# Adaptive-norm attention and spatial-shift MLP on one core: TensorE's order chosen by the state of banks and engines

## The chip, the cores and the metric

One Trainium2 chip, one of its cores. The metric is the device time of one execution in microseconds. The engines are named as the profile names them: PE (TensorE, matrix products), DVE (VectorE), ACT (ScalarE), POOL (GpSimd) and SP (SyncE, which issues the DMAs here). PE writes its results into PSUM banks, from which DVE and ACT read.

## The reference

The input x has 2048 rows of 512. A row of modulation vectors is made from c; then come an attention block with 32 heads of 16, and a mixer with a shift along the sequence, followed by an MLP of width 1792. Between them stand layer norms.

```python
mod = (silu(c) @ w_mod).reshape(1, 6, 1, -1)          # sa, ca, ga, sb, cb, gb
h = layernorm(x) * (1 + ca) + sa
q, k, v = split(h @ wqkv)                             # 32 heads of 16
x = x + ga * (softmax(q @ k.T * 16 ** -0.5) @ v) @ wo
h = layernorm(x) * (1 + cb) + sb
g = gelu(layernorm(h) @ w1)                           # tanh form
x1 = h + concat(shift(g, 1), shift(g, -1), shift(g, 2), shift(g, -2)) @ w2
x = x + gb * (x1 + gelu(layernorm(x1) @ w3) @ w4)
```

Weights are scaled up (by 8 in the attention, by 64 in the mixer), so that products are made of high and low parts: three matmuls (lines 339, 341 and 343, the helper mm3) for one exact product.

## The kernel before

All instructions are recorded in an order that a planner (class Sched) works out while the kernel is built. It keeps one modelled clock per engine (T["P"] for PE, "A" for ACT, "D" for DVE, "G" for POOL, "S" for the DMA queue), chains of dependent operations that wait for those clocks, and generators that yield PE work. On the chip each engine then takes its instructions strictly in the recorded order.

The program has three stages. First layer norm and the first keys and queries. Then a long stage in which attention runs and all other products (the rest of q, k, v; wo, w1, w2, w3, w4 for the four chunks of 512 rows) are placed between its parts. At the end what is left of the last chunk.

Attention runs over 64 units (four chunks of 512 queries by 16 pairs of heads) with 16 steps each, 1024 steps in all. Step s has two row pairs (row_pair). A row pair is two matmuls that run together on the two halves of PE's rows: sc (line 1021) for the scores of step s, and mb (line 1005), the same scores turned round, 24 steps ahead (LEAD), of which DVE takes the maximum (line 1001, mx<-mb) so that a unit's shift is known before its scores come. ACT then takes exp of sc (line 1017, pt<-sc). p_low halves the upper parts of pt, on POOL (line 1072) or, when POOL is late by the plan, in two halves on ACT (line 127). The columns (pv_part) are four matmuls at a time: with the high parts (line 1098, one for each step) and with the low parts (line 1095, one for two steps), so three parts for two steps.

sc and mb share seven PSUM banks (NSM) with the other products. A row pair takes two banks; they come free when DVE has its maximum and ACT its exp.

What sets PE's order around the change is a fixed pattern. The main loop walks over blocks of three row pairs (GRP). Each block is recorded whole: it waits until the plan has banks for all its pairs (sch.gap fills that wait with other products), then come three pairs, then, in every second block (CPER), all column parts that are two blocks back (LAG), and in the other blocks sch.fill places other products up to a budget of nanoseconds for each step (SC0, TAILB). At some steps drain forces the generators on until a key is done.

```python
    blocks = [range(32 * u + i, min(32 * u + i + GRP, 32 * u + 32)) for u in range(-2, NU) for i in range(0, 32, GRP)]
        if k >= LAG and (k % CPER == 0 or not blk):
        if k % CPER == CPER - 1 or s0 < 0:
            sch.fill(due)
```

The elementwise work of the other products also runs through the planner: a gelu is Square on ACT, cube on DVE, Tanh on ACT, prod on DVE, then a copy and a difference for the two parts on ACT and POOL; x1_add, xb_add and z_add (lines 1372, 1482, 1535) add a finished product on DVE. The factor 0.5 of gelu is put into w2 and w4 by an extra ACT copy of each of their 18 half pieces (line 899).

## Time and profile before

| what | value |
|---|---|
| median of 3 runs | 2002.66 us (2001.76 to 2005.11) |
| the profiled execution, from its first to its last instruction | 2000.7 us, mean granted clock 0.986 |
| PE busy | 1920.9 us (96%) |
| DVE busy | 1652.2 us (83%) |
| ACT busy | 1473.6 us (74%) |
| POOL busy | 1676.1 us (84%) |
| stage with rows and columns | 61.5 to 1845.6 us |

Busy time of an engine is the time in which at least one of its instructions runs. Matmuls are pipelined, and one that waits inside the pipeline counts as busy; what PE really needs is better read from the distance between the starts of its matmuls. The line number in a row leads to the code; names on both sides of the arrow are what an instruction writes and reads. A row "A <- B" of the waits says that A stood idle until B was done.

### The profile page before, as it was taken

The page shows a single profiled execution, that of the slowest core. Times are in us where ns is not written, and L with a number is a line of the kernel's source. Part 1 is how long each engine was busy: PE and PEld are TensorE (multiplying, and loading weights), DVE is VectorE, ACT ScalarE, POOL GpSimd, SP SyncE. Part 2 cuts the span into 40 slices and gives each one's busy share as a digit, 9 for nine tenths or more (in the row PEclk, how much of TensorE's full clock was granted, in tenths as well). Part 3 has the DMA queues.
Part 4 walks back from the last instruction along what each step waited for, and adds up shares of the span by engine and source line. Part 5 has one row for each costly group of instructions (what it writes and reads, how often), then busy time and mean ns, then how long its engine had stood idle before and what let it go on. Part 6 is the DMA issues. An engine that isn't in the chain of part 4 may idle for free.

```text
span 2000.7 us, 42354 instructions
## 1 busy us (share of the span) xinstructions
PE 1920.9 (96%) x14480; PEld 1146.7 (57%) x14480; DVE 1652.2 (83%) x3010; ACT 1473.6 (74%) x3083; POOL 1676.1 (84%) x1609
## 2 busy tenths in 40 slices
PE   7999999999999999999999999999999999999899
PEld 4655555555455555555455555555555555555798
DVE  7887988888899888888989898898898889883643
ACT  5376888777878777777878787786787878777443
POOL 6287999889999998888999998898899989888532
PEclk8999999999999999999999999999999999999999
DMA  5767677766643334345433333334433343334432
GB/s 184 205 201 228 182 231 218 244 225 192 198 157 111 115 103 143 109 136 162 126 111 92 109 111 114 115 119 148 157 98 100 115 151 107 121 95 147 149 146 90
DMA packets 232352, 293.24 MB, mean 147 GB/s; under 512 B 125876, under 2 KB 177076, under 8 KB 215848
## 3 DMA queue, kind: packets, MB, share of 16 engines
q1 hardware_dynamic: 232136, 290.53, 46.4%
q8 instruction: 115, 1.88, 0.4%
q14 instruction: 101, 0.83, 0.1%
HBM read 225.81 MB, written 62.91 MB: 144 GB/s over the span
## 4 chain that ended last, share of the span: by engine, by line
PE 67%; DVE 16%; ACT 8%; issue 3%; POOL 2%; DMA 2%; SPq 1%; POOLq 0%; ACTq 0%; DVEq 0%
PE mb L1005 14%; PE sc L1021 10%; PE pv L1098 10%; DVE mx L1001 9%; PE w L339 7%; PE w L343 6%; PE w L341 6%; PE pv L1095 4%; ACT pt L1017 4%; POOL pt L1072 2%; DVE xs L1421 1%; DVE sq L1418 1%; DMA vst<-Vs 1%; PE mr L644 1%; PE ot L1127 1%
## 5 line engine op out<-in xcount | busy, mean ns | idle before, releaser
L1072 POOL TENSOR_SCALAR pt<-pt 128x1024 f16<-128x1024 uint16 x988 | 1312.5, 1365 | 132.6 <-ACT pt L1017 125.4
L1001 DVE TENSOR_REDUCE mx<-mb 128x1 f32<-128x512 f32 x2048 | 1281.0, 683 | 76.0 <-PE mb L1005 54.5
L1017 ACT ACTIVATE pt<-sc 128x512 int32<-128x512 f32 x2048 | 1090.8, 606 | 272.3 <-PE mb L1005 164.9
L1005 PE MATMUL mb<-kst,qtl 64*128 64x512 f32 x2048 | 752.1, 454 | 49.0 <-ACT pt L1017 16.1
L1021 PE MATMUL sc<-qtl,kst 64*128 64x512 f32 x2048 | 716.4, 444 | 2.6 <-DVE A L329 0.6
L1005 PEld LDWEIGHTS mb<-kst,qtl 64*128 64x128 f32 x2048 | 348.7, 193 | 254.5 <-DVE mx L1001 91.4
L1021 PEld LDWEIGHTS sc<-qtl,kst 64*128 64x128 f32 x2048 | 335.6, 186 | 153.5 <-DVE mx L1001 47.1
L1098 PE MATMUL pv<-pt,vst 128*32 128x512 f16 x4096 | 358.2, 397 | 0.1
L1095 PE MATMUL pv<-pt,vst 128*17 128x512 f16 (+1 forms) x2048 | 213.7, 394 | 2.2 <-POOL pt L1072 1.7
L1098 PEld LDWEIGHTS <-vst 128*32 128x32 bf16 x4096 | 90.9, 95 | 167.6 <-issue 108.8
L339 PE MATMUL w<-A,wr 128*128 128x256 f32 (+2 forms) x576 | 175.3, 304 | 0.3 <-ACT A L333 0.3
L1428 POOL TENSOR_TENSOR g<-xs,g 128x256 fp32r<-128x256 f32 (+2 forms) x144 | 103.2, 718 | 83.4 <-ACT g L1427 81.3
L341 PE MATMUL w<-A,wr 128*128 128x256 f32 (+2 forms) x576 | 169.8, 295 | 0.5 <-DVE A L329 0.3
L343 PE MATMUL w<-A,wr 128*128 128x256 f32 (+2 forms) x576 | 167.7, 291 | 0.0
L339 PEld LDWEIGHTS w<-A,wr 128*128 128x128 f32 x576 | 109.6, 190 | 35.4 <-DVE mx L1001 10.3
L339 PE MATMUL w<-wr,g 128*128 128x512 f32 x288 | 119.2, 414 | 0.6 <-ACT g L1427 0.6
L341 PEld LDWEIGHTS w<-A,wr 128*128 128x128 f32 x576 | 109.9, 191 | 12.4 <-issue 11.3
L343 PE MATMUL w<-wr,g 128*128 128x512 f32 x288 | 114.7, 398 | 0.2 <-POOL g L1428 0.2
L341 PE MATMUL w<-wr,g 128*128 128x512 f32 x288 | 113.6, 394 | 0.0
L343 PEld LDWEIGHTS w<-A,wr 128*128 128x128 f32 x576 | 109.8, 191 | 6.7 <-issue 6.7
L1535 DVE TENSOR_TENSOR x<-x,w 128x512 f32<-128x512 f32 x64 | 43.9, 687 | 82.0 <-PE w L343 82.0
L1424 ACT ACTIVATE sq<-w 128x256 f32<-128x256 f32 (+2 forms) x144 | 55.7, 387 | 68.8 <-PE w L343 66.0
(151 smaller groups left out, 2103.8 us busy)
## 6 DMA issues: line engine op xcount, KB each, us to landing
wr<-Ws SPq DMA_DIRECT2D x80, 1024.0 KB
kst<-Ks SPq DMA_DIRECT2D x189, 256.0 KB
vst<-Vs SPq DMA_DIRECT2D x252, 192.0 KB
qtl<-Qs SPq DMA_DIRECT2D x192, 64.0 KB
Vs<-vt SPq DMA_DIRECT2D x32, 384.0 KB
Ws<-wq SPq DMA_DIRECT2D x40, 256.0 KB
Ws<-wst SPq DMA_DIRECT2D x40, 256.0 KB
wst<-in_B_w_dram SPq DMA_DIRECT2D x36, 256.0 KB
```

What stands on the lines that cost most here:

```text
L339: te.matmul(o, lh, rh, start=first, stop=False)
L341: te.matmul(o, lh, rl, start=False, stop=False)
L343: te.matmul(o, ll, rh, start=False, stop=last)
L1001: end = sch.crit("D", 605, e + PX, lambda: dve.reduce_max(mxs[u][:, j, g, c:c + 1], b, axis=AX.X))
L1005: return ready, lambda: te.matmul(b, lhs, kst[u % 3][r, c * CH:(c + 1) * CH], start=True, stop=True), after
L1017: ea = sch.crit("A", 480, e + PX, lambda: act.activation(pt[s][:, j], b, AF.Exp))
L1021: return ready, lambda: te.matmul(b, kst[u % 3][r, kt * P:(kt + 1) * P], qst[u][r], start=True, stop=True), after
L1072: e_low[s] = XP["G"] + sch.crit("G", 1345, ready, lambda: pool.tensor_scalar(o, i, 0.5, 1.0, op0=OP.mult, op1=OP.mult))
L1095: te.matmul(acc[r:r + n, :], v[:, (kt + i) % 4, c - n:c].bitcast(F16), pt[s + i].bitcast(F16)[:, j, 0::2], start=False, stop=kt == NKT - 2 ...
L1098: te.matmul(acc[r:r + 32, :], v[:, kt % 4, r:r + 32], pt[s].bitcast(F16)[:, j, 1::2], start=kt == 0, stop=False, skip_group_check=True)
L1424: sch.chain(("A", cA(n), lambda: act.activation(sq, b, AF.Square)), ("D", cD(n), cube), ("A", cA(n), lambda: act.activation(sq, sq, AF.Tan ...
L1428: ("G", cG(n), lambda: pool.tensor_tensor(lo, xs, hi, op=OP.subtract)), (None, 0, end), bank=b)
```

## The change

- The main loop has no blocks. It holds three modes for PE (r rows, c columns, o other products), and Sched.to books 95 ns for each change and 107 more for an entry into rows. At each turn it looks at the modelled banks and clocks. Inside a burst of rows (up to GRP pairs) it goes on while the next pair's banks come free within STAY (300 ns). Otherwise it reckons when banks for a whole burst are free (st) and when the engine that drains them runs dry (dry); rows start if that is not more than BACK (150 ns) away, and not while many column parts are ready or much credit for other products is left. Until then it places columns, if at least CMIN (4) parts are ready or if they fit into the time left, or else other products, while there is credit.
- Credit for other products follows DUES: pairs of a step and of the microseconds that are to be spent on them by then, 67.7 by step 20 up to 527.8 by step 1012. SC0 and TAILB go.
- p_low is recorded one pair of steps later (PLAG) and one row at a time; the second half on ACT follows after the next row.
- A unit's loads (load_unit) may come up to UWAIT (4) steps later, where the products that they read are not stored yet; before, drain forced them at once. The drain for oT at the start of a chunk becomes a wait inside o_fin, and o_fin's tiles sm and rc have one buffer more each.
- The factor 0.5 of gelu moves into the normalization ahead of w1 and w3: the variance is multiplied by 4 in an instruction that stands there already, Square and Tanh get scales of 2, and the 18 ACT copies go.
- The zero rows of qtl are copied from a tile of 4 by 128 that is read four times, where it was 4 by 512.

```diff
-SC0 = (32, 900.0, 700.0)
-TAILB = (0.0, 500.0, 560.0, 590.0)
+DUES = ((20, 67.7), (60, 87.3), (85, 95.9), (122, 115.8), (150, 130.7), (205, 149.7), (245, 167.7),
+        (505, 270.0), (765, 395.7), (1012, 527.8))
+BTOP, BLOW = 1200.0, 300.0
...
+SWITCH, ENTER = 95.0, 107.0
+EARLY, STAY, BACK, GRACE = 300.0, 300.0, 150.0, 0.0
+OWE, CTOP = 500.0, 5000.0
+CHIGH, CMIN, CMOST, PTLOW, PLAG = 2500.0, 4, 6, 2, 1
...
+    def to(self, mode):
+        if self.mode != mode:
+            self.T["P"] += SWITCH + (mode == "r") * ENTER
+            self.mode = mode
...
-            if nm in ("w2", "w4"):
-                ops.append(("A", cA(), lambda f=f: act.activation(f, f, AF.Copy, scale=0.5)))
...
+            yield lambda: not ci or ("oT", ci - 1) in done
...
-        sm = at.tile([P, 8, DH + 1], F32, name="sm", tag="sm", bufs=1)
-        rc = at.tile([P, 8, 1], F32, name="rc", tag="rc", bufs=2)
+        sm = at.tile([P, 8, DH + 1], F32, name="sm", tag="sm", bufs=2)
+        rc = at.tile([P, 8, 1], F32, name="rc", tag="rc", bufs=3)
...
-                dve.tensor_scalar(mv[:, 1:2], mv[:, 1:2], EPS, None, op0=OP.add)
+                dve.tensor_scalar(mv[:, 1:2], mv[:, 1:2], EPS, 4.0 if half else 1.0, op0=OP.add, op1=OP.mult)
...
-            sch.chain(("A", cA(n), lambda: act.activation(sq, b, AF.Square)), ("D", cD(n), cube),
-                      ("A", cA(n), lambda: act.activation(sq, sq, AF.Tanh, scale=GELU_A * GELU_C)),
+            sch.chain(("A", cA(n), lambda: act.activation(sq, b, AF.Square, scale=2.0)), ("D", cD(n), cube),
+                      ("A", cA(n), lambda: act.activation(sq, sq, AF.Tanh, scale=2.0 * GELU_A * GELU_C)),
...
+        return min(BTOP, max([BLOW] + [(1000.0 * w - sch.spent) / (d - s) for d, w in DUES if d > s]))
...
+        if asked:
+            ci, pr = units[asked[0]]
+            keys = [("kq", pr // 4)] + [("q", pr // 8)] * (ci > 0)
+            if r >= UWAIT:
+                for key in keys:
+                    drain(key)
+            if all(key in done for key in keys):
+                load_unit(asked.pop())
...
+        nc_ = cols()
+        if can:
+            if sch.mode == "r" and burst < GRP:
+                slack = one - now
+                row = slack <= STAY
+            else:
+                st = one
+                for k in range(2, GRP + 1):
+                    if need * k <= len(free) and free[need * k - 1] < LATE:
+                        st = max(st, free[need * k - 1] - (k - 1) * CROW)
+                dry = sch.T["D"] if s + LEAD < NS else sch.T["A"]
+                slack = max(st, dry - CROW - PX - EARLY) - enter - now
+                row = slack <= BACK and (sch.mode == "r" or sch.credit < CHIGH and not (nc_ >= CMIN and len(pts) <= PTLOW))
+        if not row:
+            n = 0
+            if nc_ >= CMIN or nc_ and slack >= nc_ * CCOL + (sch.mode != "c") * SWITCH:
+                do_cols(nc_)
+                n = nc_
+            else:
+                stop = now + max(slack, 0.0) + GRACE
+                while (sch.T["P"] < stop or sch.credit > CHIGH) and sch.credit > (-OVER if sch.open else 0.0) and sch.one():
+                    n += 1
...
+        if row:
+            do_row(x, max(now, one - enter))
+            burst = 1 if enter else burst + 1
+            x += 1
+            sch.credit = max(min(sch.credit + budget(s) / 2, CTOP), -OWE)
```

The numbers of instructions on PE, DVE and SP stay. In the order of the instructions the change shows at many places; three are given here. The first is PE near the end of the attention stage, before the change: from an other product (w) through two bursts of row pairs (mb and sc), with a visit to the columns (pv, each with its weights' load, of which the middle is left out) between them, to the next other product.

```order
L343 MATMUL w_27333<-wr,g_26256 128x512
L1005 MATMUL mb<-kst_153,qtl_151 128x512
L1021 MATMUL sc<-qtl_605,kst_607 128x512 x2
L1005 MATMUL mb<-kst_153,qtl_151 128x512 x2
L1021 MATMUL sc<-qtl_605,kst_607 128x512
L1098 LDWEIGHTS vst_611
L1098 MATMUL pv<-pt_614,vst_611 32x512
...
L1095 MATMUL pv<-pt_616,vst_611 25x512
L1021 MATMUL sc<-qtl_605,kst_607 128x512
L1005 MATMUL mb<-kst_153,qtl_151 128x512 x2
L1021 MATMUL sc<-qtl_605,kst_607 128x512
L339 MATMUL w_27401<-wr,g_26653 128x512
```

Five column parts stand between the first two bursts, and twelve matmuls of one other product follow the second. At the same row pairs after the change:

```order
L1036 MATMUL sc<-qtl_605,kst_607 128x512
L1110 LDWEIGHTS vst_611
...
L1113 MATMUL pv<-pt_618,vst_612 32x512
L355 MATMUL w_27526<-wr,g_27111 128x512
L357 MATMUL w_27526<-wr,g_27111 128x512
L359 MATMUL w_27526<-wr,g_27111 128x512
L355 MATMUL w_27526<-wr,g_27111 128x512
L1036 MATMUL sc<-qtl_605,kst_607 128x512
L1020 MATMUL mb<-kst_153,qtl_151 128x512 x2
L1036 MATMUL sc<-qtl_605,kst_607 128x512
```

Now a few column parts and a few matmuls of an other product stand together between two bursts, and a product is cut over several such visits.

The second place is DVE at the same time before: the maxima (mx), and the adds of the other products (x).

```order
L1535 TENSOR_TENSOR x_14268<-x_14268,w_27255 128x512
L1001 TENSOR_REDUCE mx<-mb 128x1 x6
L1535 TENSOR_TENSOR x_21727<-x_21727,w_27333 128x512
L1001 TENSOR_REDUCE mx<-mb 128x1 x5
L1535 TENSOR_TENSOR x_21729<-x_21729,w_27401 128x512
L1001 TENSOR_REDUCE mx<-mb 128x1 x6
```

And after, at the adds of the products that the PE rows above show:

```order
L1016 TENSOR_REDUCE mx<-mb 128x1 x5
L1554 TENSOR_TENSOR x_13684<-x_13684,w_27486 128x512
L1016 TENSOR_REDUCE mx<-mb 128x1 x3
L1554 TENSOR_TENSOR x_21194<-x_21194,w_27526 128x512
L1016 TENSOR_REDUCE mx<-mb 128x1 x6
L1153 TENSOR_REDUCE sm<-ot 128x136
L1554 TENSOR_TENSOR x_21196<-x_21196,w_27562 128x512
```

An add stood after every fifth or sixth maximum; the distances are now less regular.

The third place is ACT in the first quarter, at the exps (pt<-sc) of about the same steps, before:

```order
L1017 ACTIVATE pt_620<-sc 128x512
L127 ACTIVATE pt_618<-pt_618 128x512
L900 ACTIVATE wq_120<-wst_116 128x512
L1017 ACTIVATE pt_620<-sc 128x512
L127 ACTIVATE pt_618<-pt_618 128x512
L1017 ACTIVATE pt_613<-sc 128x512 x2
```

And after:

```order
L1032 ACTIVATE pt_617<-sc 128x512 x2
L140 ACTIVATE pt_616<-pt_616 128x512
L914 ACTIVATE wq_120<-wst_117 128x512
L1032 ACTIVATE pt_618<-sc 128x512
L140 ACTIVATE pt_616<-pt_616 128x512
L349 ACTIVATE qk_165<-k 128x512
```

A halving on ACT comes two steps after its exp in both, in two halves with other work between them; over the program there are 120 such halves where there were 72, and POOL has 964 halvings where it had 988.

More of the change, by code (lines that the diff above doesn't have):

```diff
@@ new lines, in fillers, with do_cols, do_row @@
+    def fillers():
+        for e in "ADG":
+            sch.misc(e, max(sch.T["P"], sch.T[e]) + TOLE[e])
+    def do_cols(n):
+        sch.to("c")
+        for y in pvs[:n]:
+            if not y[1]:
+                e_hi.pop(y[0])
+            pv_part(*y)
+        del pvs[:n]
+    def do_row(x, t):
+        sch.T["P"] = t
+        sch.to("r")
+        late = sorted(e_exp)
+        one_row(x)
+        for q in late:
+            if 2 * q < x - 2 * PLAG:
+                p_low(q)
+    x, end, seen, burst = -2 * LEAD, 2 * NS, -99, 0
@@ L1632 @@
-        sch.gap(start)
-        sch.flush(need)
-        sch.T["P"] = max(sch.T["P"], start) + CIN
-        low = sorted(e_exp)
-        for s, i in row:
-            for fn in row_pair(s, i):
-                fn()
+        can = x < end
+        if can:
+            s, i = divmod(x, 2)
+            if x == LENDS:
+                sch.most = MOST
+            if i == 0 and seen != s:
+                seen = s
+                before(s)
+                if s >= 0 and s % 16 == 0:
+                    drain(("shift", s // 16))
+            can = i or s < 0 or bool(pts)
@@ L1639 @@
+        now, row, slack = sch.T["P"], False, LATE
+        if can:
+            need = (s >= 0) + (s + LEAD < NS)
+            sch.flush(need)
+            free = sorted(sm.t)
+            one = free[need - 1 + 2 * (s < 0)]
+            if one >= LATE:
+                one = free[need - 1]
+            enter = (sch.mode != "r") * (SWITCH + ENTER)
+        else:
+            for q in sorted(e_exp):
+                p_low(q)
             while second:
                 second.pop(0)()
-        while second:
-            second.pop(0)()
```

117 lines of the change are left out of this document (51 added, 66 removed).

## The prediction

> **What bounds the kernel now.** I began with the page's busy shares and its chain, to see whether one engine sets the end.
>
> ```profile
> span 2000.7 us, 42354 instructions
> PE 1920.9 (96%) x14480; PEld 1146.7 (57%) x14480; DVE 1652.2 (83%) x3010; ACT 1473.6 (74%) x3083; POOL 1676.1 (84%) x1609
> PE 67%; DVE 16%; ACT 8%; issue 3%; POOL 2%; DMA 2%; SPq 1%; POOLq 0%; ACTq 0%; DVEq 0%
> ```
>
> PE looks full at 96%, yet the chain is PE's for only 67%: a matmul counts as busy while it waits in the pipeline. So the second view is PE's timeline in a clean place, read from start to start.
>
> ```profile
> start us, us, engine line op out<-in xcount [idle before <-releaser]
> 704.83 0.66 PE L1127 MATMUL ot<-ident,ac 128*128 128x128 f32 x4
> 705.24 0.50 PE L339 MATMUL w<-wr,g 128*128 128x512 f32 x1
> ...
> 1752.21 0.28 PE L339 MATMUL w<-A,wr 128*128 128x256 f32 x1
> 1752.33 0.28 PE L341 MATMUL w<-A,wr 128*128 128x256 f32 x1
> ...
> 1790.35 0.39 PE L341 MATMUL w<-wr,g 128*128 128x512 f32 x1
> 1790.58 0.39 PE L343 MATMUL w<-wr,g 128*128 128x512 f32 x1
> 1790.89 0.50 PE L1005 MATMUL mb<-kst,qtl 64*128 64x512 f32 x1
> 1790.90 0.72 PE L1021 MATMUL sc<-qtl,kst 64*128 64x512 f32 x2
> 1791.24 0.61 PE L1005 MATMUL mb<-kst,qtl 64*128 64x512 f32 x2
> 1791.47 0.39 PE L1021 MATMUL sc<-qtl,kst 64*128 64x512 f32 x1
> 1791.80 0.41 PE L1098 MATMUL pv<-pt,vst 128*32 128x512 f16 x4
> 1792.03 0.41 PE L1095 MATMUL pv<-pt,vst 128*17 128x512 f16 x4
> 1792.26 0.64 PE L1098 MATMUL pv<-pt,vst 128*32 128x512 f16 x8
> 1792.72 0.42 PE L1095 MATMUL pv<-pt,vst 128*17 128x512 f16 x4
> 1793.07 0.50 PE L1021 MATMUL sc<-qtl,kst 64*128 64x512 f32 x1
> ```
>
> Here are PE's real prices. A row pair (mb and sc, which run together) takes 0.23 us (1791.24 to 1791.47), a column part (four pv) 0.23, another product 0.23 with 512 columns, 0.12 with 256, 0.10 with 128. A change between the three kinds costs more: other to rows 0.31 (1790.58 to 1790.89), rows to columns 0.33, columns to rows 0.35, so about 0.10 beyond the work. And after each entry into rows the second pair comes 0.35 after the first, another 0.11.
>
> Third, the stage and pieces of it. All row and column work lies between 61.5 and 1845.6 us.
>
> ```profile
> core 0: us, PE busy (x) PEld busy (x) DVE busy (x) ACT busy (x) POOL busy (x), PEclk, DMA share, GB/s
> 61.50:1845.60 1784.10, 1730.71 (x13482) 988.78 (x13484) 1531.93 (x2769) 1382.19 (x2899) 1579.23 (x1472) 0.99 0.48 146
> 112.00:1809.50 1697.50, 1646.73 (x12920) 936.37 (x12918) 1476.90 (x2669) 1327.89 (x2777) 1524.52 (x1418) 0.99 0.47 145
> 334.70:401.20 66.50, 61.86 (x432) 34.86 (x431) 54.81 (x83) 49.79 (x100) 55.12 (x47) 0.95 0.72 229
> 520.20:564.00 43.80, 40.72 (x330) 18.89 (x328) 40.92 (x71) 38.50 (x78) 40.96 (x36) 1.00 0.47 147
> 1651.20:1700.20 49.00, 48.40 (x414) 28.06 (x412) 45.14 (x85) 41.54 (x92) 47.56 (x44) 1.00 0.36 104
> 1700.20:1755.40 55.20, 54.82 (x439) 32.71 (x437) 46.78 (x85) 40.13 (x86) 46.44 (x42) 1.00 0.37 116
> 1809.50:1845.60 36.10, 35.22 (x294) 19.15 (x292) 9.77 (x21) 32.38 (x70) 35.33 (x35) 1.00 0.32 105
> ```
>
> By the order PE holds in that stage 2096 row slots (478 us at those prices), 1536 column parts (347), 3178 other matmuls (1062, 1480 and 636 with 512, 256 and 128 columns, 487), and 1361 changes of kind with 631 second pairs after an entry (207). That is 1519 of 1784.1 us, so PE stands still for about 265. DVE (1532) and POOL (1579) are as loaded as PE. The four rows of single pieces each hold 64 row pairs, and there are 31 such pieces from 112 to 1809.5. In 520.2 to 564.0 hardly any other product is left to place: PE needs 30, POOL (41.0) and DVE (40.9) fill the 43.8. In 1651.2 to 1700.2 POOL bounds (47.56 of 49.0), 1.4 are lost. In 1700.2 to 1755.4 PE bounds: 14.6 rows, 10.8 columns, 18.9 others, 7.2 changes, together 51.5 of 55.2, 3.7 lost. In 334.7 to 401.2 it needs 52.7 of 66.5. If I take for each piece the largest need of the four engines (counts of the order by row durations, scaled so that the whole gives the row 112 to 1809.5), the 31 pieces sum to 1566. The other 131 us are lost inside pieces, to bad timing.
>
> Fourth, who waits for PE on DVE, between 112 and 1810:
>
> ```profile
> DVE mx L1001 <- PE mb L1005: 50.9, 101, 2.0
> DVE x L1535 <- PE w L343: 47.4, 36, 1.9
> DVE mx L1001 <- PE sc L1021: 15.4, 32, 1.6
> DVE xb L1482 <- PE w L343: 10.5, 11, 1.5
> DVE x L1372 <- PE wo L343: 8.9, 12, 1.5
> 1791.00 0.69 DVE L1535 TENSOR_TENSOR x<-x,w 128x512 f32<-128x512 f32 x1 [1.50 <-PE w L343]
> ```
>
> Sum 133 us: for 66 DVE has no new bank of maxima, for 67 it stands before an add whose product PE has not finished. The last line is the pattern in small: during PE's twelve products before 1790.89 DVE is idle for 1.50 us.
>
> **The change, part by part.**
>
> Changes of kind. The new order has 1928 in place of 1361: 722 visits to rows (634), 635 to columns (352), 572 to other products (376). 567 times 0.10 is 57, and 709 second pairs in place of 631 give 78 times 0.11, or 9: **+66 us of PE time**. How much reaches the end depends on the piece. The Trainium skill, page "TensorEngine Tiling (Array Packing)", Key Properties, says that changing the tiling mode drains TensorE, and speaks so against this change; the trace agrees (64-row, 32-column and whole-array matmuls meet at those 0.10 us). The page "TensorE: Matmul & The Clock Gate", Single matmul latency, gives a lone matmul a fixed part of about 166 ns; at that price the 567 changes would be, as an estimate from that page, 94 us in place of 57.
>
> The bound of the pieces. The other products are spread more evenly: 14 to 21 us in most pieces, where before they ran from 9 to 21; the ends of chunks stay poor (four pieces with 1 to 7 us now, two with 1 and 5 before). PE's need over the 31 pieces rises from 1435 to 1511 (66 for changes, the rest other products moved forward out of the last stretch), DVE's from 1477 to 1483; POOL's falls from 1525 to 1499. The largest needs then sum to 1573 where they were 1566: **+7 us**, not 66, since in 21 of the 31 pieces PE was not the bound. It is in 15 now.
>
> The halving of pt (p_low) is part of this:
>
> ```profile
> L1072 POOL TENSOR_SCALAR pt<-pt 128x1024 f16<-128x1024 uint16 x988 | 1312.5, 1365 | 132.6 <-ACT pt L1017 125.4 <-ACT mf L1052 1.7 <-POOL pt L1072 1.1
> L127 ACT ACTIVATE pt<-pt 128x512 f16<-128x512 uint16 x72 | 57.8, 808 | 0.0
> L899 ACT ACTIVATE wst<-wst 128x512 f32<-128x512 f32 x18 | 11.7, 650 | 0.0
> ```
>
> POOL has 964 (24 fewer, 33 us off), ACT 120 halves (48 more, 39 us on). ACT, at 1328 of 1697.5, covers it; only one piece (row pairs 256 to 319) becomes ACT's, in the sum above. Without that cover it would cost at most the 39.
>
> The last stretch, 1809.5 to 1845.6, has no maxima. It loses 10 us of other products (PE need 37 before, 25 now), and ACT with 32.38 busy becomes the bound: at least 0, at most 8 off, **-5** taken, near what ACT leaves.
>
> The loss inside pieces. Rows now start when banks are about to come free and DVE is about to run dry, and other products come in shorter visits: 8.5 matmuls a visit before, 5.6 now, 34% less. DVE's 66 us without a bank should shrink by that, 23; the 67 us before unfinished adds I take at half that rate, 11, because the add still stands where the planner expects the product: **-34**. Bounds: the best is every piece at the 1.4 us of the POOL-bound row, 31 times 1.4 is 43 of the 131 left, -88. The worst is that nothing improves and 5 more pieces, PE's now, lose 3.7 in place of 1.4, +12.
>
> Edits that I cost at nothing. The 18 ACT copies by 0.5 (11.7 us, L899) go; they lie in the first third, where ACT is the least loaded; 0, at best -12. The 4.0 and 2.0 ride in operands of instructions that stay. A unit's loads of qtl and kst may come up to 4 steps later on SP's queue (a step is 1697.5/1000, 1.7 us) and are then still 4 steps, 7 us, ahead of their first maxima; late they would hold one burst each, in the first quarter only, at most 16 units. The zero rows are written with 512-byte pieces, and sm and rc get a buffer more: queues and engines with slack there, 0. The stages before 61.5 and after 1845.6 keep their order (180 and 794 matmuls).
>
> Sum: +7 - 5 - 34 = -32, against the profiled execution, of which the page gives the span alone, 2000.7. The median of the runs, 2002.7, lies 2.0 above that, so I forecast **1971 us**.
>
> **The rivals.** *PE becomes the bound (slower).* In 15 pieces the changes are paid in full; if bad timing is not the fixed pattern's doing but that of a plan which counts DVE's other work too short (cD gives 0.60 us for the add that the timeline shows at 0.69), the loss stays. Then +7 - 5 + 12 = +14: 2017. It decides once the loss falls by less than 2 us. For it: PE's and DVE's needs are nearly equal in the new pieces (1511 and 1483), and the PE-bound row loses more than the POOL-bound one. Against: the row where PE bounds loses it in the long visits that go. The two pages named above belong beside this case.
>
> *The state finds nearly all (much faster).* All pieces come near the POOL-bound row: +7 - 5 - 88, or 1917; half way from my forecast, 1944. For it: the first eight pieces lose 48 us, as 334.7 to 401.2 shows. Against: that row has DMA at 0.72 and the clock at 0.95, which no order changes.
>
> *It does nothing.* DVE's waits move from rows to other products, the loss stays and the PE-bound pieces keep theirs: +7 - 5, 2005, or with a small gain the old time.
>
> **How the numbers follow.** Forecast 0.52, with its own range 1945 to 1995; much faster 0.10; nothing 0.09; PE-bound 0.29. A difference of 0.2%, 4 us, is about what a measurement of this kernel can tell. Faster 0.62, same 0.09, slower 0.29. The range that leaves out no more than 2 in 10 reaches from 1930, most of the way into the much faster case, to 2022, past the slower one's 2017.
>
> **What would show it.** Right: DVE's waits for PE fall from 133 to about 99 while PE's changes of kind rise; the stage of 1784 shortens to about 1752 with DVE and POOL busier by share; pieces like 334.7 to 401.2 lose most of their 14 us. POOL has 964 and ACT 120 halvings. Wrong: late pieces (1651 on) grow to 55 us and more with PE waiting at mb for DVE as before; DVE's 67 us at adds grow, since an add waits for a product cut into three visits; or the start of the stage waits for late units.

## The result, and the profile after

The change made the kernel slower. Its median was 2024.51 us (2020.83 to 2026.45, 4 runs) beside 2002.21 us (1995.28 to 2005.11, 4 runs) of the kernel before on the same chip. The ratio on record is 1.0119, 95% interval 1.0096 to 1.0141 (the two medians alone give 1.0111). The forecast was 1971 us. The chips of the experiments differ a little (before's median lies between 1995 and 2002 us on them), so below only ratios to before on the same chip are compared, and traces.

The page of the kernel after, its span, its busy shares and its chain:

```profile
span 2019.0 us, 42344 instructions
PE 1958.0 (97%) x14480; PEld 1133.0 (56%) x14480; DVE 1676.2 (83%) x3010; ACT 1495.4 (74%) x3113; POOL 1652.2 (82%) x1585
PE 76%; DVE 13%; ACT 5%; POOL 2%; issue 2%; DMA 1%; SPq 1%; POOLq 0%; ACTq 0%; DVEq 0%
```

The chain went through PE for 67% of the span, and now does for 76%; ACT's share fell from 8% to 5%. The stage and pieces of it, with the same row pairs as in the rows of before (row pairs are counted from the program's first, at 61.50 before and 62.40 after):

```profile
core 0: us, PE busy (x) PEld busy (x) DVE busy (x) ACT busy (x) POOL busy (x), PEclk, DMA share, GB/s
62.40:1863.90 1801.50, 1767.20 (x13486) 973.47 (x13486) 1555.57 (x2769) 1404.00 (x2929) 1556.48 (x1448) 1.00 0.47 145
114.90:1829.00 1714.10, 1688.36 (x12987) 928.35 (x12985) 1504.88 (x2680) 1348.79 (x2809) 1507.29 (x1400) 1.00 0.46 145
352.10:407.60 55.50, 55.08 (x417) 28.85 (x416) 49.50 (x80) 45.82 (x90) 49.83 (x42) 1.00 0.81 264
513.90:556.30 42.40, 41.24 (x342) 19.66 (x340) 41.53 (x73) 38.38 (x78) 40.56 (x36) 1.00 0.57 187
556.30:621.00 64.70, 62.18 (x447) 34.17 (x444) 56.60 (x111) 52.49 (x106) 55.66 (x69) 1.00 0.29 91
988.70:1054.70 66.00, 64.53 (x457) 35.67 (x455) 56.98 (x112) 52.38 (x105) 57.16 (x69) 0.97 0.30 90
1662.50:1718.00 55.50, 55.50 (x427) 30.57 (x425) 47.17 (x82) 38.98 (x83) 46.63 (x42) 1.00 0.42 135
1718.00:1774.70 56.70, 56.40 (x449) 33.11 (x445) 48.60 (x88) 42.41 (x94) 49.14 (x45) 1.00 0.33 104
1829.00:1863.90 34.90, 28.36 (x224) 11.57 (x224) 4.71 (x10) 33.43 (x68) 29.18 (x28) 0.95 0.23 73
```

The stage grew from 1784.1 to 1801.5 us (+17.4). It begins 0.9 later, and what follows it takes 155.1 us in both. So the whole loss lies in the stage, as the span shows it (18.3).

The piece of the first quarter (66.5 before) is now 55.5: that part of the forecast came. But much of it was one stop of PE, not many small losses. Before, PE waits once for a maximum, and the granted clock falls to half for 6.8 us from 349.1 on:

```profile
349.18 0.79 PE L1005 MATMUL mb<-kst,qtl 64*128 64x512 f32 x1 [3.51 <-DVE mx L1001]
```

The runs e8 and e9 below have before's order here, and again one distance of 4.0 us between two matmuls and a clock of 0.95 in this piece; after, e10 and e11 have no such stop and 1.00. The clock of this piece thus went with the order, which the prediction had excluded. The late piece that POOL had bound at 49.0 is now 55.5 with PE at 55.50; the one that PE had bound went from 55.2 to 56.7. And the two pieces that follow the ends of chunks, rows 556.30 and 988.70, stood in before as:

```profile
564.00:620.30 56.30, 53.95 (x400) 28.57 (x396) 51.48 (x98) 43.98 (x85) 51.78 (x60) 1.00 0.44 143
993.70:1049.30 55.60, 52.96 (x390) 28.07 (x388) 50.06 (x95) 44.14 (x85) 50.53 (x58) 0.97 0.33 103
```

They got 47 and 67 more matmuls and grew by 8.4 and 10.4 us. By quarters of the stage (512 row pairs each, the first with what lies before pair 64) the state's order gained 7.3 us in the first and lost 4.0, 16.0 and 5.7 in the others; the last stretch won 1.2. By the account below, the price of the changes rose by 20 to 23 us in every quarter, while PE's waits fell by 30, 20, 16 and 12. The third quarter also got 11 us more of other products, and the last stretch 10 fewer, where PE then waits 10 us more.

A stretch of PE in a late piece of the kernel after, from start to start:

```profile
1690.19 0.50 PE L1020 MATMUL mb<-kst,qtl 64*128 64x512 f32 x1
1690.19 0.73 PE L1036 MATMUL sc<-qtl,kst 64*128 64x512 f32 x2
1690.54 0.62 PE L1020 MATMUL mb<-kst,qtl 64*128 64x512 f32 x2
1690.77 0.39 PE L1036 MATMUL sc<-qtl,kst 64*128 64x512 f32 x1
1691.09 0.41 PE L1110 MATMUL pv<-pt,vst 128*17 128x512 f16 x4
1691.33 0.64 PE L1113 MATMUL pv<-pt,vst 128*32 128x512 f16 x8
1691.90 0.50 PE L359 MATMUL w<-wr,g 128*128 128x512 f32 x1
1692.23 0.40 PE L355 MATMUL w<-wr,g 128*128 128x512 f32 x1
1692.47 0.40 PE L357 MATMUL w<-wr,g 128*128 128x512 f32 x1
1692.79 0.49 PE L1036 MATMUL sc<-qtl,kst 64*128 64x512 f32 x1
```

From 1690.19 to 1692.79 there are three row pairs, three column parts and three other products, nine times 0.23, or 2.07 us of work, and PE waits for nobody; yet it takes 2.60. The rest, 0.53, is price: three changes of kind, the second row pair (0.35 after the first), and one thing that the prediction left out: the *second* other product comes 0.33 after the first (1691.90 to 1692.23), the third 0.24 after that. An entry into other products costs another 0.10, as an entry into rows does. Before shows it as well, 0.34 to the second matmul and 0.22 to the third:

```profile
1787.95 0.50 PE L339 MATMUL w<-wr,g 128*128 128x512 f32 x1
1788.29 0.39 PE L341 MATMUL w<-wr,g 128*128 128x512 f32 x1
1788.51 0.39 PE L343 MATMUL w<-wr,g 128*128 128x512 f32 x1
```

The planner does not book it either (SWITCH and ENTER are for changes and rows).

PE's whole account of the stage, from the starts of all its matmuls (work at the durations of the prediction, 7 us more than there, since the stage has 3246 other products and not 3178; price: changes, second row pairs and 0.10 for each entry into two or more other products; waits: all that is left, and so also what a lower granted clock costs), in us:

| kernel | changes | work | price | waits | stage | ratio to before, 95% |
|---|---|---|---|---|---|---|
| before | 1361 | 1319 | 243 | 222 | 1784 | 1 |
| after | 1928 | 1319 | 327 | 155 | 1802 | 1.0119 (1.0096 to 1.0141) |
| e1, state, column visits of 4 parts and more | 1476 | 1319 | 262 | 250 | 1831 | 1.0270 (1.0253 to 1.0287) |
| e2, e1 with longer visits to others | 1368 | 1319 | 245 | 262 | 1826 | 1.0244 (1.0228 to 1.0259) |
| e3, fixed pattern, short | 1903 | 1319 | 318 | 221 | 1858 | 1.0416 (1.0398 to 1.0433) |
| e4, fixed, the change's due dates | 1361 | 1319 | 243 | 242 | 1803 | 1.0145 (1.0130 to 1.0160) |
| e5, state, before's budgets | 1852 | 1319 | 314 | 190 | 1823 | 1.0213 (1.0187 to 1.0238) |
| e6, state, even due dates | 1926 | 1319 | 327 | 155 | 1801 | 1.0089 (1.0064 to 1.0113) |
| e7, fixed, even due dates | 1383 | 1316 | 247 | 229 | 1792 | 1.0087 (1.0063 to 1.0110) |
| e8, before with the small edits | 1361 | 1319 | 243 | 217 | 1779 | 0.9993 (0.9975 to 1.0010) |
| e9, before, two matmuls a product | 1361 | 1263 | 243 | 236 | 1742 | 0.9714 (0.9687 to 0.9740) |
| e10, after, two matmuls a product | 1926 | 1263 | 324 | 180 | 1767 | 0.9833 (0.9806 to 0.9859) |
| e11, state in the first quarter alone | 1512 | 1318 | 266 | 200 | 1784 | 1.0006 (0.9992 to 1.0020) |
| e12, state, before's spending course | 1906 | 1319 | 323 | 216 | 1859 | 1.0373 (1.0350 to 1.0396) |
| e13, fixed, the change's spending course | 1292 | 1319 | 229 | 271 | 1820 | 1.0187 (1.0165 to 1.0210) |
| e14, e12 with column visits of 2 parts and more | 1691 | 1319 | 293 | 212 | 1824 | 1.0211 (1.0187 to 1.0235) |
| e15, state, column visits of 2 parts and more | 1653 | 1319 | 289 | 211 | 1819 | 1.0224 (1.0201 to 1.0246) |
| e16, state, entry into others booked | 1973 | 1319 | 333 | 156 | 1808 | 1.0150 (1.0126 to 1.0174) |
| e17, state, rows 400 ns earlier | 1953 | 1319 | 331 | 160 | 1811 | 1.0158 (1.0136 to 1.0181) |
| e18, e15 and e17 together | 1673 | 1319 | 291 | 227 | 1837 | 1.0340 (1.0316 to 1.0365) |

The change raises PE's price by 84 us and takes 67 us of its waits away. That is the +17. The account is of one profiled execution each, which lies up to 6 us from the median that its ratio rests on. Of the 67 us, 12 are granted clock: for 38 us of the stage before and 14 after the profile grants half the clock, and half of that is lost.

### The profile page after: what moved, and what is told of

It is laid out like the page before. It is cut to its first block, busy times and chain, and to the rows that moved or that the text cites. A ratio compares the mean times of both kernels' runs of the same rounds, so it can differ in the third digit from the quotient of the medians.

```text
span 2019.0 us, 42344 instructions
## 1 busy us (share of the span) xinstructions
PE 1958.0 (97%) x14480; PEld 1133.0 (56%) x14480; DVE 1676.2 (83%) x3010; ACT 1495.4 (74%) x3113; POOL 1652.2 (82%) x1585
## 4 chain that ended last, share of the span: by engine, by line
PE 76%; DVE 13%; ACT 5%; POOL 2%; issue 2%; DMA 1%; SPq 1%; POOLq 0%; ACTq 0%; DVEq 0%
PE mb L1020 14%; PE sc L1036 11%; PE pv L1113 10%; DVE mx L1016 9%; PE w L355 8%; PE w L359 7%; PE w L357 7%; PE pv L1110 7%; ACT pt L1032 2%; POOL pt L1087 1%; PE ot L1145 1%; PE v L355 1%; PE xT L1223 1%; PE q L355 1%; PE v L357 1%
## 5 line engine op out<-in xcount | busy, mean ns | idle before, releaser
L1016 DVE TENSOR_REDUCE mx<-mb 128x1 f32<-128x512 f32 x2048 | 1295.7, 683 | 160.9 <-PE mb L1020 126.2
L1087 POOL TENSOR_SCALAR pt<-pt 128x1024 f16<-128x1024 uint16 x964 | 1281.3, 1362 | 126.1 <-ACT pt L1032 122.7
L1020 PE MATMUL mb<-kst,qtl 64*128 64x512 f32 x2048 | 733.5, 448 | 22.1 <-DVE mx L1016 7.9
L1020 PEld LDWEIGHTS mb<-kst,qtl 64*128 64x128 f32 x2048 | 343.5, 192 | 196.8 <-DVE mx L1016 69.7
L1113 PEld LDWEIGHTS <-vst 128*32 128x32 bf16 x4096 | 116.5, 94 | 117.5 <-issue 67.2
L355 PE MATMUL w<-A,wr 128*128 128x256 f32 (+2 forms) x576 | 174.6, 303 | 2.0 <-ACT pt L1032 1.3
L357 PE MATMUL w<-A,wr 128*128 128x256 f32 (+2 forms) x576 | 171.9, 298 | 0.5 <-DVE A L345 0.3
L359 PE MATMUL w<-A,wr 128*128 128x256 f32 (+2 forms) x576 | 171.8, 298 | 0.0
L1110 PEld LDWEIGHTS <-vst 128*17 128x17 f16 (+1 forms) x2048 | 54.0, 90 | 144.2 <-issue 135.1
L355 PE MATMUL w<-wr,g 128*128 128x512 f32 x288 | 120.8, 419 | 0.7 <-ACT g L1446 0.6
L359 PE MATMUL w<-wr,g 128*128 128x512 f32 x288 | 119.1, 413 | 0.2 <-POOL g L1447 0.2
L357 PE MATMUL w<-wr,g 128*128 128x512 f32 x288 | 118.5, 412 | 0.0
```

The costliest lines, as they stand in the source:

```text
L355: te.matmul(o, lh, rh, start=first, stop=False)
L357: te.matmul(o, lh, rl, start=False, stop=False)
L359: te.matmul(o, ll, rh, start=False, stop=last)
L1016: end = sch.crit("D", 605, e + PX, lambda: dve.reduce_max(mxs[u][:, j, g, c:c + 1], b, axis=AX.X))
L1020: return ready, lambda: te.matmul(b, lhs, kst[u % 3][r, c * CH:(c + 1) * CH], start=True, stop=True), after
L1087: e_low[s] = XP["G"] + sch.crit("G", 1345, ready, lambda: pool.tensor_scalar(o, i, 0.5, 1.0, op0=OP.mult, op1=OP.mult))
```

## The experiments

The expectations weigh these theories, by letters. A, later P: PE pays its changes in full, or nearly so, and that is the loss. B: the due dates lose it, since they give the other products to the wrong pieces; Q at first is the same for where they are placed. C: the choice by state itself is at fault, PE's time is not the bound. D: each piece takes the largest need of the four engines and a few microseconds more. In the last four runs, Q is that waits come back when visits get longer, and T that rows reach DVE late because the plan lacks the 0.10 us at an entry into others.

**Fewer or more changes: e1, e2, e3.** e1 leaves out column visits of under four parts; e2 also lets visits to other products run 400 ns longer and records waiting halvings ahead of the columns, which the diff leaves out; e3 is the kernel before with columns and other products after every block.

```diff
-            if nc_ >= CMIN or nc_ and slack >= nc_ * CCOL + (sch.mode != "c") * SWITCH:
+            if nc_ >= CMIN or nc_ and not can:                       # e1, e2
-EARLY, STAY, BACK, GRACE = 300.0, 300.0, 150.0, 0.0
+EARLY, STAY, BACK, GRACE = 300.0, 300.0, 150.0, 400.0               # e2
-CPER = 2
+CPER = 1                                                            # e3, in before
```

> The changed kernel, but columns are taken only in visits of at least four parts (or when no rows can go on); everything else as in the change. Changes of kind on PE by the order: 1476 in place of 1928 (before: 1361). Theory A (PE is the bound and pays every change of kind, about 0.10 us, and another 0.10 us at the second piece after an entry into rows or into other products): the price falls from 329 to 264 us, so the time falls by 65 us less what longer visits give back to waits, at most a half: 1960 to 1992 us. Theory B (the due dates put other products in the wrong places): no difference, 2018 to 2030 us. Theory C (the choice by modelled state itself times rows badly): 2010 us or more.

> As the run with columns in visits of at least four parts, and other products go on for 400 ns longer once they have begun (GRACE). 1368 changes of kind, as many as before the change (1361), but still chosen by state. Theory A: price 246 us, as before the change (244); what remains is what the choice by state saves in waits, 30 to 60 us of the 69 that it saved: 1945 to 1975 us. If rows come too late by the longer visits and DVE runs dry, 1985. Theory B: 2018 to 2030 us. Theory C: 2010 us or more.

> The kernel before, with columns and other products after every block of three row pairs in place of every second (CPER 1): the fixed pattern with 1903 changes of kind, no choice by state. Theory A: price 320 us in place of 244, +76, less what the more even mixture saves in waits, at most the 69 that the change saved: 2009 to 2075 us, slower than before. Theory C (short visits are good, the choice by state is what loses): faster than before, 1940 to 1995 us.

e1 and e2 were slower than the change, 1.0270 and 1.0244, though their price is 65 and 82 us lower: waits rose by 95 and 107. So the number of changes alone does not set the time. e3, with nearly as many changes as the change has (1903), was much slower, 1.0416: its price is the change's (318), its waits are those of before (221). So a fixed pattern cut as fine saves no waits on the whole, where the change saves 66 us (221 to 155). Not all of that is the choice by state, since e3 and the change also differ in what paces the other products. e5 below has the choice by state with the budgets of e3: waits of 190 us at 1852 changes, 31 less than e3, of which 14 are e3's waits for a DMA (qtl<-nm) that e5 doesn't have.

**Pattern and due dates crossed: e4, e5, e6, e7.** e4 is before with the change's DUES and budget, e5 is after with before's SC0 and TAILB; e6 and e7 have the last three due dates replaced by one, so that the spending is even.

```diff
+        return min(BTOP, max([BLOW] + [(1000.0 * w - sch.spent) / (d - s) for d, w in DUES if d > s]))   # e4, e7, in before
+        return 900.0 if s < 32 else 700.0 if s < NS // NC else TAILB[min(s * NC // NS, NC - 1)]          # e5, in after
-        (505, 270.0), (765, 395.7), (1012, 527.8))
+        (1036, 527.8))                                                                                   # e6, e7
```

> The kernel before with the due dates of the change in place of its two tables of budgets; the fixed pattern stays, 1361 changes of kind. Theory A: near the time before, 1990 to 2012 us. Theory B (the due dates lose the time): 2015 to 2030 us.

> The changed kernel with the two tables of budgets of the kernel before in place of the due dates; the choice by state stays. 1852 changes of kind (after: 1928). Theory B (the due dates alone lose the 1.2%): back to the time before, ratio to before 0.985 to 1.003. Theory D (the time is the sum over pieces of 64 row pairs of the largest need of an engine, and about 3 to 4 us a piece beside it; what matters is where other products lie): the needs sum to 1613 us here, 1608 in the change, 1579 before, since these budgets spend the work still earlier and leave the ends of chunks empty: ratio 1.010 to 1.022.

> The changed kernel with due dates that run evenly from step 245 to step 1036 (167.7 to 527.8 us), so that 10 us of other products stay for the last stretch, where DVE has no maxima, in place of 2. 1926 changes of kind. Theory D: the needs sum to 1597 us in place of 1608, the last stretch takes 3 to 5 us more: 6 to 8 us faster than the change, ratio to before 1.006 to 1.010. Theory A (every change of kind is paid in full and nothing else counts): as the change, 1.010 to 1.014. Theory B (any due dates lose): 1.010 to 1.014.

> The kernel before with due dates as in the even run (167.7 us by step 245, 527.8 by step 1036) in place of its budgets; fixed pattern, 1383 changes of kind. Theory D: needs 1571 us (before 1579, with the due dates of the change 1594), last stretch 45 in place of 38: as before, ratio 0.995 to 1.004. Theory B (due dates as such lose): 1.010 to 1.016, as in the run with the due dates of the change.

| | before's budgets | the change's due dates | even due dates |
|---|---|---|---|
| fixed pattern | 1 | 1.0145 | 1.0087 |
| choice by state | 1.0213 | 1.0119 | 1.0089 |

Each part alone is slower than before, by 1.45% and 2.1%, and together they lose 1.2%: they don't add. With even due dates both orders take the same time, the one by 80 us more price, the other by 74 us more waits. D's ranges held for e5 and e6, not for e7 (0.995 to 1.004). So B holds in part (in the fixed pattern the dates cost 1.45% with the very same changes), and C in its plain form, that the choice by state loses whatever paces it, does not. The mean granted clock was lower in e4 and e7 (0.984 and 0.985) than in before's runs on the same chips (0.990 and 0.989), and not in e5 and e6. Among before's runs there, 0.001 of the clock goes with 0.8 and 1.7 us, so 4 to 5 of the 29 us that e4 loses and 6 of the 18 of e7 go with it (an estimate).

**The small edits: e8.** Before with gelu's 0.5 in the normalization and the zero rows from the smaller tile, as in the change's diff, nothing else.

> The kernel before with only gelu's 0.5 moved into the normalization (the 18 ACT copies gone) and the zero rows read from the 4 by 128 tile. All theories: no difference, ratio 0.997 to 1.003. If these edits cost something of the 1.2%, 1.004 or more.

0.9993 (0.9975 to 1.0010): they cost and bring nothing, as forecast.

**What a microsecond of PE is worth: e9, e10.** In before and in after, the third matmul of every product with wo, w2 and w4 is left out; the planner books its time as before, so that the order of everything else is kept.

```diff
-            for _ in mm3(b, lhs(k, 0), lhs(k, 1), wh[:, k % 2], wl[:, k % 2], k == 0, k == nk - 1):
-                yield nsq(CH)
+            te.matmul(b, lhs(k, 0), wh[:, k % 2], start=k == 0, stop=False)
+            yield nsq(CH)
+            te.matmul(b, lhs(k, 0), wl[:, k % 2], start=False, stop=k == nk - 1)
+            yield nsq(CH)
+            yield nsq(CH)
```

> The kernel before with the third matmul (low part by high part) left out of the products with wo, w2 and w4: part of the result is missing. The planner's costs and the order of all else stay. PE loses 54 us of work between 112 and 1809 us and 24 us after the attention stage. Theory D: the largest needs of the 31 pieces fall by 31 us, since 10 pieces have PE as their bound; the attention stage gets 25 to 38 us shorter, the end 20 to 24. Theory C (PE is not the bound, DVE and POOL are): the stage gets less than 15 us shorter.

> The changed kernel with the same third matmuls left out (part of the result is missing); order and planner's costs stay. PE loses 59 us of work between 115 and 1829 us. Theory D: PE bounds 19 pieces, the needs fall by 40 us; the attention stage gets 35 to 50 us shorter, so more than the kernel before does, the end 20 to 24. Theory C: the stage gets less than 15 us shorter.

The windows from row pair 64 to 2048, e9 first, then e10, where before has 1697.50 and after 1714.10:

```profile
112.60:1767.40 1654.80, 1597.24 (x12684) 894.68 (x12682) 1476.57 (x2670) 1327.78 (x2777) 1524.33 (x1418) 0.99 0.48 149
```
```profile
113.60:1791.80 1678.20, 1648.85 (x12741) 889.21 (x12737) 1501.40 (x2680) 1348.59 (x2809) 1504.96 (x1400) 1.00 0.47 148
```

In the whole stage 56 us of PE work less shorten before by 42 us (1784 to 1742) and after by 35 (1802 to 1767): 0.75 and 0.62 us for each. DVE, ACT and POOL do the same work in 112.60 to 1767.40 as in before (1476.57, 1327.78 and 1524.33, to a microsecond). So PE's time counts in before as well, where by the sums of the prediction other engines bound 21 of 31 pieces. That excludes C's claim that PE's time does not matter. D had put more in the change (35 to 50) than in before (25 to 38), and it is the other way round; of the 24 us taken out behind the stage 17 and 16 came back, where D had 20 to 24.

The pieces of 64 row pairs say more. All that e9 takes out of the stage lies from row pair 576 on. In 9 pieces of before PE has the largest need (from the trace, entries counted): there 30.8 us were taken out, and the pieces got 29.2 shorter. In the 8 others from which work was taken, POOL or DVE has the largest need: 23.9 us were taken out, and they got 9.2 shorter. The 14 pieces that lost no work are 4.4 us shorter together. So PE's time came back at 0.95 where PE has the largest need, and at 0.39, not at nothing, where another engine has it.

**Where the gain is: e11.** After up to row pair 544 of the kernel's count (592 in the count of the windows), then the fixed pattern, with budgets of 520, 600 and 640 ns; the fixed loop is put behind the new one.

```diff
-    x, end, seen, burst = -2 * LEAD, 2 * NS, -99, 0
-    while x < end or pvs or acs:
+    XS = 544
+    x, end, seen, burst = -2 * LEAD, XS, -99, 0
+    while x < end:
...
+    LAG, CPER, CARRY, TAILB = 2, 2, 3000.0, (0.0, 520.0, 600.0, 640.0)
```

> The choice by state and the due dates only up to row pair 544, just past the first quarter, where the change was 5 to 9 us faster; from there the fixed pattern of before, with budgets of 520, 600 and 640 ns a step for the last three quarters. 1512 changes of kind. Theory D: needs 1562 us (before 1579), the last stretch 6 longer, the loss of the first quarter as in the change (10 less): 12 to 24 us faster than before, ratio 0.988 to 0.994. Theory A (price of the changes in full: 267 in place of 244): ratio 1.005 to 1.012.

The first quarter, from the first row to pair 512, in before, after and e11:

```profile
61.50:520.20 458.70, 440.12 (x3204) 253.84 (x3206) 384.42 (x654) 342.82 (x716) 383.12 (x329) 0.97 0.72 219
```
```profile
62.40:513.90 451.50, 438.98 (x3217) 247.61 (x3217) 386.92 (x656) 348.28 (x721) 374.05 (x321) 0.99 0.73 225
```
```profile
62.90:515.30 452.40, 439.99 (x3217) 247.74 (x3217) 385.86 (x656) 348.00 (x721) 374.64 (x321) 0.98 0.73 224
```

The gain of the first quarter, 7 us, is there again (6.3), and yet the kernel ends with before, 1.0006: its third quarter gained 8.8 us, its fourth lost 8.9 and the last stretch 4.8, as the spending of the new budgets came out. Neither D's range nor A's holds it. It is no version that beats both.

**The course of the spending: e12, e13, e14.** e12 is after with due dates at every 16 steps that copy the course of before, and e13 before with the course of after; both look at the next date alone. e14 is e12 with column visits of at least two parts.

```diff
+DUES = ((16, 67.7), (32, 72.0), (48, 83.6), ... (1008, 512.6), (1048, 532.0))      # e12, e14; e13 with the other course
+        return min(BTOP, max(0.0, next(((1000.0 * w - sch.spent) / (d - s) for d, w in DUES if d > s), 300.0)))
```

> The choice by state, but the due dates are the kernel before's own course: what it had spent on other products at every 16th step, and only the next due date counts. 1906 changes of kind (1361 before), other products lie within 4 us a piece where before has them. Theory P (price: 326 us of changes and second pieces in place of 244, each us of PE worth 0.6 to 0.8 by the two runs with matmuls left out, less what the choice saves in waits, which left +17 in the change): as slow as the change, ratio to before 1.008 to 1.014. Theory Q (placement decides): as before, 0.995 to 1.003.

> The fixed pattern, with due dates that are the changed kernel's own course (spent at every 16th step, only the next one counts). 1292 changes of kind. Theory P: price 230 us in place of 244: ratio 0.992 to 1.000. Theory Q: as slow as the change, 1.010 to 1.015.

> As the choice by state with the course of before, but columns in visits of at least two parts: 1691 changes of kind, price 295 us, 31 less. Theory P: 31 times 0.6 to 0.8 is 18 to 25 us off, less longer waits, which in the run with at least four parts ate all of 65 and 25 more: between 12 us faster and 6 slower than the choice with the course of before. Theory Q: within 4 us of it.

Both e12 and e13 were slower than what they were made from, 1.0373 and 1.0187. e12 should have been near before by placement, or near after by price, and is far above both; e13 has fewer changes than before and loses 1.9%. Neither theory in its pure form gives this. But e12 does not try them cleanly. Half of what its waits exceed the change's (216 for 155) are three stops of PE of 10 us each, which no other state order has (the sum of them, then the first):

```profile
PE sc L1035 <- DMA qtl<-nm: 29.5, 3, 10.4
```
```profile
455.33 1.73 SPq L118 DMA_DIRECT2D qtl<-Qs  x3
...
460.38 5.02 SPq L118 DMA_DIRECT2D qtl<-nm  x8
464.74 0.76 PE L1035 MATMUL sc<-qtl,kst 64*128 64x512 f32 x1 [9.48 <-DMA qtl<-nm]
```

At each of them SP issues the loads of a unit, after a wait for PE, and only behind them the transfers (qtl<-nm) on which the next row stands. The granted clock, too, is lower in e12 and e13 (0.980 and 0.983, before 0.989 on the same chip). What else costs time in e13, and whether budgets that look one date ahead do, is not shown. e14 is 1.6 points, or 33 us, faster than e12, more than either theory allowed; but it has none of the three stops, so that this is not the worth of its price (293 for 323) alone.

**The visits and the plan's clock: e15 to e18.** All in after.

```diff
-            if nc_ >= CMIN or nc_ and slack >= nc_ * CCOL + (sch.mode != "c") * SWITCH:
+            if nc_ >= CMIN or nc_ >= 2 and slack >= nc_ * CCOL + (sch.mode != "c") * SWITCH or nc_ and not can:   # e15, e18
-            self.T["P"] += SWITCH + (mode == "r") * ENTER
+            self.T["P"] += SWITCH + (mode != "c") * ENTER                                                        # e16
-EARLY, STAY, BACK, GRACE = 300.0, 300.0, 150.0, 0.0
+EARLY, STAY, BACK, GRACE = 700.0, 300.0, 150.0, 0.0                                                              # e17, e18
```

> The change with one rule altered: outside the end, columns go in only where at least two parts are ready (a visit of one part is not made). It has 1653 changes of kind where the change has 1928, which at 0.10 us for a change, 0.11 for a second row pair and 0.10 for a second other product is 38 us less time of PE. Theory P (PE's time is what the change lost, and a microsecond of it is worth 0.6 to 0.8 as the runs without the third matmul showed): 23 to 30 us faster than the change, so 1994 to 2001, a ratio of 0.998 to 1.001 to the kernel before, if no wait grows. Theory Q (the waits that the short visits remove are worth as much as the changes cost, so that the sum stands still, as with the even due dates, where both orders took the same time): the waits come back, ratio 1.008 to 1.016. The run with visits of at least four parts had 1.027, the one with two parts and the spending course of before won 1.6 points over one part.

> The change, but the planner's clock books the 107 ns for the second matmul at each entry into other products too, which the traces show and the change's plan leaves out. Theory T (rows come late for DVE because the modelled clock of PE runs ahead of the chip at each of the 572 visits): DVE's waits for a bank of maxima fall from 152 us to below 125, and the ratio falls from 1.012 to 1.000 to 1.006. Theory P (PE's own time is the loss): 1973 changes in place of 1928 are 6 us more time of PE, so the ratio stays at 1.012 to 1.016 whatever DVE waits for.

> The change with rows started 400 ns earlier against the time at which DVE runs dry by the plan (EARLY 700 in place of 300 ns). Theory T (rows come late for DVE): DVE's waits for a bank of maxima fall from 152 to about 110 us, ratio 1.000 to 1.006. Theory P: 1953 changes, 4 us more time of PE, and the rows then wait for banks in place of DVE for rows; ratio 1.010 to 1.016.

> Both of the last edits: column visits of at least two parts, and rows started 400 ns earlier; 1673 changes. If P and T both hold in part the two gains add and this is the best of the state orders: ratio 0.990 to 1.000. If P alone holds: as the run with column visits of two parts, within 0.003. If neither: 1.008 to 1.016.

e15 was 1.0224, above even Q's range: 38 us of price went (327 to 289), and 56 us of waits came (155 to 211). The place of these waits is seen at the weights' loads of mb, which stand in line on PE ahead of a row and wait there for a bank. The groups of these loads (busy and mean ns, then the idle time ahead of them and what ended most of it) in before, after, e15 and e1:

```profile
L1005 PEld LDWEIGHTS mb<-kst,qtl 64*128 64x128 f32 x2048 | 348.7, 193 | 254.5 <-DVE mx L1001 91.4
```
```profile
L1020 PEld LDWEIGHTS mb<-kst,qtl 64*128 64x128 f32 x2048 | 343.5, 192 | 196.8 <-DVE mx L1016 69.7
```
```profile
L1020 PEld LDWEIGHTS mb<-kst,qtl 64*128 64x128 f32 x2048 | 345.6, 192 | 222.2 <-DVE mx L1016 85.2
```
```profile
L1020 PEld LDWEIGHTS mb<-kst,qtl 64*128 64x128 f32 x2048 | 350.6, 192 | 245.4 <-DVE mx L1016 122.2
```

The change takes 58 us off the idle time there and 22 off the part that DVE's maxima end; each step back to longer column visits gives some of it back. The starts say where in a burst: at its third and later row pairs PE waits 136 us before, 62 after, 103 in e15 and 127 in e1. (e3, which ends its bursts after three, has 70 there, but 67 us more than before ahead of and behind its column visits.) My reading is that a single column part fills the time until a bank comes free, and that without it PE stands at the row.

T fell: e16 (1.0150) and e17 (1.0158) are no faster than the change, and DVE's waits for banks of maxima stayed at 149 and 158 us. Both lie where P had put them (6 and 4 us more price, waits as before), though e17's loss sits in one piece: row pairs 64 to 128 took 74.1 us in place of 63.0. e18 adds up to nothing better: 1.0340, above all three of its ranges.

## Why the prediction was wrong

**The counts and prices per change were right**: 1928 changes, +65 us for changes and second row pairs in the trace (207 to 273), where +66 was forecast. What was missing is the entry into other products: 544 in place of 354 at 0.10, +19 us. The price is +84. It stands in the timeline from which I quoted (1787.95 to 1788.29); I read the 0.23 from the third product on and didn't ask for the second.

**The step that failed is "+7 us, not 66, since in 21 of the 31 pieces PE was not the bound".** Two things were wrong in it. The entries were missing from the price: with them, and counted from the trace, the prediction's own sum of the largest needs rises by 29 (1579 to 1608), not by 7. And a larger need of another engine was taken as full cover: in such pieces e9 gives 0.39 us for each of PE's, and 0.75 over the stage. That inside a piece PE bounds some stretches and DVE or POOL others, and that what PE loses in the first is not given back in the second, is my reading of the 0.39. At 0.62 to 0.75 (e10 and e9) the 84 us are worth +52 to +63, by rates that were measured on work taken out, not on changes put in.

**The loss inside pieces, -34.** By the prediction's own sum it fell by 12 only (119 to 106); together with the needs, +29, that is the +17 of the 31 pieces. Counted the other way, with the price at +52 to +63, the gain must have been 35 to 46, and PE's waits fell by 67, 12 of them with the clock. So waits did shrink, on PE, at the third and later row pairs of its bursts; how much of that the forecast may claim depends on the count. On DVE, where I had looked for it, they did not. DVE's waits from row pair 64 to 2048 after:

```profile
DVE mx L1016 <- PE mb L1020: 124.1, 267, 2.2
DVE mx L1016 <- PE sc L1036: 27.7, 51, 2.2
DVE x L1554 <- PE w L359: 0.3, 1, 0.3
```

Before, 66 us stood at maxima and 67 at adds (47.4, 10.5 and 8.9). Now the adds wait 0.3 us, and maxima wait 152 us, in 318 waits of half a microsecond. The sum rose from 133 to 152; 99 was forecast. Shorter visits did not give DVE its banks sooner, nor ACT: its waits for PE at the exps rose from 245 to 294 us. That PE comes to the rows late because it is full, as in the stretch from 1690.19, is my reading; e16 and e17 only show that neither the plan's missing 0.10 nor an earlier start by the plan changes it.

**The last stretch**: -5 forecast, -1.2 measured (36.1 to 34.9), with ACT at 33.43 of 34.90 as its bound, as named.

**The edits at nothing**: gelu's factor and the zero rows were right (e8). The late units cost the change little (PE waits 2.3 us for qtl<-nm, the stage begins 0.9 us later), but they were not tried alone, nor were the later halvings and the buffers of sm and rc. The halvings are 964 and 120:

```profile
L1087 POOL TENSOR_SCALAR pt<-pt 128x1024 f16<-128x1024 uint16 x964 | 1281.3, 1362 | 126.1 <-ACT pt L1032 122.7
L140 ACT ACTIVATE pt<-pt 128x512 f16<-128x512 uint16 x120 | 97.4, 816 | 0.0
```

**The rival** "PE becomes the bound", at 2017, is what happened, in direction and nearly in size (2024.5), and one sign of a wrong forecast came in part: a late piece grew past 55 us (row 1662.50), but PE waits less at mb for DVE than before, and the 67 us at adds went in place of growing. Its working was not the right one, though: it took the price at +7 and let the loss grow by 12, where in truth a large price meets a large gain. A rule of the Trainium skill spoke for it: page "TensorEngine Tiling (Array Packing)", Key Properties, has it that changing the mode drains TensorE. The trace agrees, with 0.10 us at each change; another 0.10 to 0.11 comes at the second unit of work behind it, on rows and on whole-array products; I named the rule and then let the sum over pieces take its weight away.

What stays open: how the 1.2% divides between order and due dates. The crossed runs show that both count and that they don't add; e12 and e13, which were to part them, brought costs of their own, e12 its three stops. That the price is what makes the change slower is so by the account, but each run with fewer changes (e1, e2, e15) got its price back in waits and more. That the measured worth of PE's work also holds for changes of kind was not tried by itself. And of fixed patterns with fewer changes than 1361 there is only e13, whose due dates differ too; longer blocks were not tried.

## What to carry to other kernels

Before an engine's added time is counted as covered, measure or bound what its time is worth now: take some of its work out with the order kept (e9) and see how much the end moves. A sum of "the largest need" over pieces does not say that the other engines' time is free: here PE's was worth 0.39 where another engine had the larger need. And when an order is cut finer, count the price at every place where a visit begins, the second instruction of it included, and set it against PE's waits: here 84 us against 67, and of the mixtures of shorter and longer visits that were run none beat the kernel before.

## What the runs showed that I had not expected

An entry into whole-array products costs 0.10 us at its second matmul beyond the 0.10 of the change (mean of 354 entries in before 0.096, of 544 in after 0.101; from the third on 2 to 3 ns; where the visit begins with transposes, ot, 0.06). So a visit of two or more units to rows costs about 0.21 us, to other products 0.20, to columns 0.10 to 0.11. A column visit is the cheap filler, and taking the shortest of them away made the kernel slower each time with the change's due dates (e1, e15, e18), while e14 was faster than e12, whose three stops it did not have.
